# Attention with cached keys: every full matmul and transpose written as two of 64 output columns

## The chip, the cores and the metric

One core of a Trainium2 chip. The metric is the time of one execution on the device in microseconds; the kernel before takes 453.37 us (median of three runs, 451.6 to 454.62). Only the core's own engines work: TensorE (PE: matmuls, and its weight loads, PEld), VectorE (DVE), ScalarE (ACT), GpSimd (POOL, set-up only) and SyncE (SP, which issues all DMAs).

## The reference

```python
B, Sq, D = 8, 112, 640;  H, Sk, Dh = 32, 512, 192          # all bf16
q = (x @ wq).reshape(B, Sq, H, Dh).transpose(0, 2, 1, 3)
scores = jnp.einsum("bhqd,bhkd->bhqk", q, k_cache) * (Dh ** -0.5)
p = softmax(scores, axis=-1)
o = jnp.einsum("bhqk,bhkd->bhqd", p, v_cache)
return o.transpose(0, 2, 1, 3).reshape(B, Sq, H * Dh) @ wo
```

Eight batches of 112 queries, 32 heads, 512 cached keys and values of 192 elements per head.

## The kernel before

**Tiles and steps.** The heads are done in two halves of 16, and a (half, batch) is a time t, 16 in all. A step n (0 to 63) is four heads of one time. For each step TensorE does five things: the queries of two head pairs that a later step needs (`q_fill`, L329: weights `wq`, 224 columns of x streamed, that is two batches), the scores (`scores`), the transposes of the softmaxed probabilities (`transposes`, L447, eight per pair of heads), the values (`values`), and a part of the output projection (`o_half`, L520: weights `wo`, 224 columns streamed). Heads of 192 are cut as 128 + 64. For the scores, the 128-deep part are the matmuls of L384 and L386 (256 keys streamed, 112 output columns), and the 64-deep rests are L397 and L399, which use the two row halves of the array side by side. For the values, the 128-wide part is L486 (112 queries streamed), and the 64-wide rests are L475, for which the two heads of a pair use the two column halves of the array side by side: one writes partitions 0 to 63 of a PSUM bank, the other 64 to 127.

**Other uses of TensorE.** x and the keys of times 0 and 1 come in their natural order and are transposed on TensorE (`x_transposes` L281, `k_transposes` L295); the keys of later times are transposed by the DMA that loads them. The end of the program has its own pieces of the output projection (`o_six` L559, `o_last` L583) and transposes the result back (`o_final` L608). `idle` (L318) runs 22 matmuls on zeros at the start.

**Who reads the results.** ACT copies queries, half of the transposed probabilities and the values out of PSUM and computes the exponentials (L417); DVE finds the maxima of the scores (L412), normalizes (L421), copies the other half of the transposes (L453) and adds up the output projection (L536, L538).

**The order.** Nothing is scheduled by the machine. Each engine has a list of operations by name (`Plan.order`), written out by hand for the front (steps 0 to 8) and the tail (from step 58) and made by a loop between (steps 9 to 57). In the loop TensorE's list of a step n is: scores of n, values of n - 2, queries, first part of the output projection, transposes of n - 1, second part. Each operation names what it depends on. `Plan.run` turns the dependences into waits on semaphores: an operation adds one to its engine's semaphore when its last instruction ends, and readers wait for a count. An operation may also name two semaphores; `emit` then returns two instructions, each of which adds to one of them. Before the change that is so for the rests of the scores alone (`St`, L402: semaphores `PE` and `PE2`), whose two last matmuls run side by side.

**The matmul in the program.** Each `e.matmul(out, weights, moving)` and each `e.transpose(out, in, identity)` becomes two instructions of TensorE: a weight load and a matmul. No weights are used twice in a row.

Of the kernel before, what the change touches and what calls it, by code (L numbers as in the profile page):

```python
# [52 lines left out]
def build_mha_kernel(nc, x, k_cache, v_cache, wq, wo, out):  # L53
# [27 lines left out]
    with ExitStack() as es:  # L81
# [40 lines left out]

        P = Plan()
        add, order = P.add, P.order


        def k_done(t, lo, hi):
# [150 lines left out]
        def x_transposes(c, bank, eng):  # L278
            def emit(e):
                for dc in range(DC):  # L280
                    mm = e.transpose(psb[:, bank, dc * 128:(dc + 1) * 128], xn[c // 4][:, c % 4, dc * 128:(dc + 1) * 128],  # L281
                                     ident[:, :])
                return mm

            def evac(e):
                dst = xT_sb[:, :, c * 128:(c + 1) * 128]
                src = psb[:, bank, 0:D].rearrange("p (c s) -> p c s", c=DC)
                return e.activation(dst, src, ACTF.Copy) if eng == "ACT" else e.tensor_copy(dst, src)
            add("PE", ("XT", c), [x_piece[c]], emit)
            add(eng, ("evX", c), [("XT", c)], evac)  # L290

        def k_transposes(t, u, bank, eng):
            def emit(e):
                for c in range(6):
                    mm = e.transpose(psb[:, bank, c * 128:(c + 1) * 128], kn[:, u, c * 128:(c + 1) * 128], ident[:, :])  # L295
                return mm

            def evac(e):
                dst = kt[t][:].rearrange("p a m c -> p (a m) c")[:, :, u * 128:(u + 1) * 128]
                src = psb[:, bank, 0:768].rearrange("p (c r) -> p c r", c=6)  # L300
                return e.activation(dst, src, ACTF.Copy) if eng == "ACT" else e.tensor_copy(dst, src)
            add("PE", ("KT", t, u), [kn_of[t, u]], emit)
            add(eng, ("evK", t, u), [("KT", t, u)], evac)


# [15 lines left out]
        def q_fill(m, lp, part, bank):  # L321
            half, bp = divmod(m, B // 2)
            blocks = (0, 1) if part == "a" else (2,)

            def emit(e):
                for j, c in enumerate(blocks):
                    for dc in range(DC):
                        c0 = lp * 2 * DH + 128 * c
                        mm = e.matmul(ps[:, bank, j * S2:(j + 1) * S2], wq_sb[:, dc, c0:c0 + 128],  # L329
                                      xT_sb[:, dc, bp * S2:(bp + 1) * S2], start=(dc == 0), stop=(dc == DC - 1))  # L330
                return mm

            def evac(e):
                n = len(blocks)
                return e.activation(q_home(m, lp)[:, blocks[0]:blocks[0] + n, :],  # L335
                                    ps[:, bank, 0:n * S2].rearrange("p (c s) -> p c s", c=n), ACTF.Copy)

            old = []
            if m != 1 and q_seq.index((m, lp)) >= NQ:
                for n in q_last(*q_seq[q_seq.index((m, lp)) - NQ]):  # L340
                    old += [("St", n, 3), ("qc", n)]
            rows = range(bp * S2 // 128, (bp * S2 + S2 - 1) // 128 + 1)
            add("PE", ("Q" + part, m, lp), [wq_piece[half, lp]] + [("evX", c) for c in rows], emit)
            add("ACT", ("evQ" + part, m, lp), [("Q" + part, m, lp)] + old, evac)

        def q_of(n):
# [20 lines left out]
        def scores(n):  # L367
# [10 lines left out]
            for j in range(2):  # L378
                def emit(e, j=j):
                    for h in range(2):  # L380
                        i = 2 * j + h
                        ev, od = (raw(j, 0), qh[:, n % 2, j, 1, :]) if h == 0 else (qh[:, n % 2, j, 2, :], raw(j, 2))
                        hs = slice(h * 256, (h + 1) * 256)
                        e.matmul(ps[0:SQ, 2 * j, hs], ev, ktb[:, :, 0, cs(i)], start=(h == 0), stop=False,  # L384
                                 skip_group_check=True)
                        mm = e.matmul(ps[0:SQ, 2 * j + 1, hs], od, ktb[:, :, 2, cs(i)], start=(h == 0), stop=False,  # L386
                                      skip_group_check=True)
                    return mm
                add("PE", ("Sm", n, j), [("qc", n), ("smax", n - 1, 2 * j), ("smax", n - 1, 2 * j + 1)] +
                    ([("evK", t, 4 * s + i) for i in range(4)] if t < 2 else [k_piece[t, s]]), emit)  # L390
            for i in range(4):
                def emit(e, i=i):
                    j, h = divmod(i, 2)
                    ev, od = ((raw(j, 1)[0:64], qh[64:128, n % 2, j, 0, :]) if h == 0 else
                              (qh[0:64, n % 2, j, 3, :], raw(j, 1)[64:128]))
                    hs = slice(h * 256, (h + 1) * 256)
                    m1 = e.matmul(ps[0:SQ, 2 * j, hs], ev, ktb[0:64, :, 1, cs(i)], start=False, stop=True,  # L397
                                  skip_group_check=True)
                    m2 = e.matmul(ps[0:SQ, 2 * j + 1, hs], od, ktb[64:128, :, 1, cs(i)], start=False, stop=True,  # L399
                                  skip_group_check=True)  # L400
                    return m1, m2
                add("PE", ("St", n, i), [], emit, ("PE", "PE2"))  # L402

        def softmax(n):
            for i in range(4):
# [34 lines left out]
        def transposes(n, j):  # L440
            bank = end_bank.get(("PT", n, j), 4 + j)

            def emit(e):
                for h in range(2):
                    for q in range(4):
                        c = (4 * h + q) * SQ
                        mm = e.transpose(psb[:, bank, c:c + SQ], p_sb[:, (4 * n + 2 * j + h) % 8, q * 128:(q + 1) * 128],  # L447
                                         ident[0:SQ, 0:SQ])
                return mm

            def evac(e):
                dst, src = pT_sb[:, j, :, :].rearrange("p h c -> p (h c)"), psb[:, bank, 0:8 * SQ]
                return e.activation(dst, src, ACTF.Copy) if j == 0 else e.tensor_copy(dst, src)  # L453
            add("PE", ("PT", n, j), [("norm", n, 2 * j), ("norm", n, 2 * j + 1)] +
                ([("smax", n, i) for i in range(4)] if n == NN - 1 else []), emit)
            add("DVE" if j else "ACT", ("evPT", n, j), [("PT", n, j)] + ([] if n - 1 in BY_DMA else [("PVm", n - 1, j)]), evac)

        def values(n):
# [22 lines left out]
            for j in range(2):  # L481
                def mains(e, j=j):
                    for h in range(2):
                        for q in range(4):
                            d0 = QJ[q] * DH + 64 * h
                            mm = e.matmul(ps[:, b0 + j, 2 * h * SQ:(2 * h + 1) * SQ],  # L486
                                          vtb[:, h0 + 2 * j + h, d0:d0 + 128], pT(j, h, q),
                                          start=(q == 0), stop=(q == 3))
                    return mm
                add("PE", ("PVm", n, j), [], mains)  # L490

            u = t // 2 * 2 + s // 2

# [17 lines left out]
        def o_half(u, f, part):  # L511
# [5 lines left out]

            def emit(e):
                for j, m, k in todo:
                    mm = e.matmul(ps[:, o_bank(u, f), j * S2:(j + 1) * S2], wo_sb[:, KU * (u % 2) + k, m * 128:(m + 1) * 128],  # L520
                                  oT_sb[:, u % NO, k, :], start=(k == 0), stop=(k == KU - 1))
                return mm
            deps = []
            if part == 0 and f == 0:
                deps = ready(u) + [("WO", half, u % 2)]
            add("PE", ("O", u, f, part), deps, emit)

        def o_acc(u, f):
            half, bp = divmod(u // 2, B // 2)
# [23 lines left out]
        def o_six(g, part):  # L553

            def emit(e):
                for k in range(18, KB) if part else range(18):
                    w, o = wo_k(k)
                    for j, m in enumerate(SIX[g]):
                        mm = e.matmul(ps[:, end_bank["O6", g, 0], j * SQ:(j + 1) * SQ], w[:, m * 128:(m + 1) * 128], o[:, 0:SQ],  # L559
                                      start=(k == 0 and j == 0), stop=(k == KB - 1), skip_group_check=True)  # L560
                return mm
            add("PE", ("O6", g, part), [("evPV", step_of[NT - 2, 2 + part])], emit)

        def o_six_acc(g):
            m0, n = SIX[g][0], len(SIX[g])
# [8 lines left out]
        def o_last(s, part):  # L574
# [3 lines left out]
            def emit(e):  # L578
                for k in range(6 * s, 6 * s + 6):
                    w, o = wo_k(k)  # L580
                    for m in blocks:
                        bank, c = LAST[m]
                        mm = e.matmul(ps[:, bank, c * SQ:(c + 1) * SQ], w[:, m * 128:(m + 1) * 128], o[:, SQ:S2],  # L583
                                      start=(k == 0 and c == 0), stop=(k == KB - 1), skip_group_check=True)
                return mm
            add("PE", ("OL", s, part), [("evPV", step_of[NT - 1, s])], emit)

        def o_last_acc(part):
            def emit(e):
# [12 lines left out]
        def o_final(b):  # L602
# [2 lines left out]

            def emit(e):
                for m in range(DC):
                    mm = e.transpose(psb[0:SQ, bank, m * 128:(m + 1) * 128], oF[:, bp, m, bb * SQ:(bb + 1) * SQ, 0],  # L608
                                     ident[:, :])
                return mm  # L610

            def evac(e):
                return e.activation(xT_sb[0:SQ, b % DC, 0:D], psb[0:SQ, bank, 0:D], ACTF.Copy)
            need = [("oacc", 8 + 2 * bp + 1, f) for f in range(4)] if bp < BL else [("oaccL", 0), ("oaccL", 1)] if bb else [("oacc6", g) for g in range(3)]
            add("PE", ("OF", b), need, emit)
            add("ACT", ("oout", b), [("OF", b), ("Qb", NM - 1, LP - 1), ("OUT", b - DC)], evac)


# [322 lines left out]
```

## Time and profile before

| | |
|---|---|
| median of three runs | 453.37 us |
| the profiled execution's own time | 452.17 us |
| its span, first to last instruction | 450.2 us |
| granted TensorE clock | 0.999 |
| TensorE: matmuls, weight loads | 6,345 and 6,345 |
| idle time of DVE, of ACT | 82 us, 112 us |
| data moved by DMA | 121.94 MB, mean 271 GB/s |

How to read the profile. "PE" rows are matmuls, "PEld" rows weight loads; both belong to one engine with one sequencer. A form such as `128*64 128x112` means 128 rows and 64 columns of the array in use, and an output of 112 streamed columns. Matmuls are pipelined: a single one is shown 0.2 us long or longer, but the next one starts much earlier. What a matmul costs in a row of many is therefore the distance from one start to the next, and in a merged line of the order of time ("x16") it is the line's length, less one matmul's own, divided by the number less one. `[0.39 <-issue]` is idle time ahead of an instruction for which the profile shows no semaphore. In a table of stretches the columns are the stretch, its length, the busy time of PE, PEld, DVE, ACT and POOL with their instruction counts, the granted clock, the DMA share and GB/s. In the DMA part a queue has its packets, megabytes, and share of 16 engines' time; "instruction" is the kind of a queue that brings an engine's program. The trace also holds every single DMA packet with queue, start, duration and size.

### The profile page before, as it was taken

To read this page: it belongs to the slowest core of one execution; us is meant where nothing else is said; L and a number is where in the kernel's file an instruction comes from. 1 tells how busy PE (TensorE), PEld (TensorE's weight loads), DVE (VectorE), ACT (ScalarE), POOL (GpSimd) and SP (SyncE) were. 2 spreads that over 40 slices of the span, in tenths; PEclk is the share of its full clock that TensorE was granted. 3 is DMA by queue.
4 is the path that set the end of the run, shared out by engine and by line. 5 is a ranking of instruction groups with operands and counts; after the bars stand their busy time and mean duration, and the time that the engine had idled before them with its cause. 6 is when DMAs were issued, how large, how long until landed. Compare 5 with 4: busy or idle time off the path is not lost.

```text
span 450.2 us, 15025 instructions
## 1 busy us (share of the span) xinstructions
PE 438.4 (97%) x6345; PEld 402.8 (89%) x6345; DVE 367.8 (82%) x1172; ACT 338.4 (75%) x787; POOL 0.7 (0%) x6
## 2 busy tenths in 40 slices
PE   8999999999999999999999999998999999999996
PEld 7799888998998899999999999997999989999986
DVE  1788789979888988898898888887798888889961
ACT  3688898868767877787687778767678777867683
POOL 0000000000000000000000000000000000000000
PEclk9999999999999999999999999999999999999999
DMA  8999999999999999999999999999999999999972
GB/s 296 373 376 359 238 302 245 250 328 277 261 275 279 315 240 352 232 336 258 274 290 232 287 229 341 261 261 363 227 306 187 276 220 217 273 244 269 223 193 67
DMA packets 232547, 121.94 MB, mean 271 GB/s; under 512 B 182560, under 2 KB 232480, under 8 KB 232480
## 3 DMA queue, kind: packets, MB, share of 16 engines
q1 hardware_dynamic: 232480, 120.99, 110.6%
q8 instruction: 50, 0.82, 0.7%
q14 instruction: 17, 0.14, 0.1%
HBM read 73.50 MB, written 1.15 MB: 166 GB/s over the span
## 4 chain that ended last, share of the span: by engine, by line
PE 85%; DMA 6%; DVE 4%; ACT 4%; issue 1%; SPq 0%; DVEq 0%; ACTq 0%
PE ps L329 18%; PE ps L520 17%; PE ps L486 11%; PE ps L447 10%; PE ps L397 7%; PE ps L475 6%; PE ps L384 6%; PE ps L386 6%; DMA wo_sb<-in_wo_dram 3%; DVE s_sb L412 3%; ACT p_sb L417 2%; PE ps L295 2%; DMA wq_sb<-p_sb 1%; DMA wq_sb<-in_wq_dram 1%; PE ps L583 1%
## 5 line engine op out<-in xcount | busy, mean ns | idle before, releaser
L417 ACT ACTIVATE p_sb<-s_sb,nmx 112x512 bf16<-112x512 f32 x256 | 183.2, 716 | 83.2 <-DVE s_sb L412 79.7
L412 DVE TENSOR_SCALAR_CACHE_REDUCE s_sb<-ps 112x512 f32<-112x512 f32 x256 | 167.5, 688 | 40.4 <-ACT p_sb L417 19.4
L329 PE MATMUL ps<-xT_sb,wq_sb 128*128 128x224 bf16 x960 | 111.1, 259 | 0.6 <-issue 0.4
L520 PE MATMUL ps<-oT_sb,wo_sb 128*128 128x224 bf16 x840 | 96.6, 259 | 1.8 <-DMA wo_sb<-in_wo_dram 1.8
L329 PEld LDWEIGHTS ps<-xT_sb,wq_sb 128*128 128x128 bf16 x960 | 88.6, 98 | 2.1 <-issue 0.9
L421 DVE TENSOR_SCALAR p_sb<-p_sb,rinv 112x512 bf16<-112x512 bf16 x256 | 79.3, 350 | 3.9
L520 PEld LDWEIGHTS ps<-oT_sb,wo_sb 128*128 128x128 bf16 x840 | 78.3, 98 | 2.1 <-DMA wo_sb<-in_wo_dram 2.1
L335 ACT ACTIVATE qr<-ps 128x448 bf16<-128x448 f32 (+1 forms) x112 | 49.1, 442 | 15.7 <-PE ps L329 15.6
L447 PE MATMUL ps<-ident,p_sb 112*128 112x112 bf16 x944 | 57.2, 213 | 1.2 <-ACT oT_sb L496 0.9
L453 ACT ACTIVATE pT_sb<-ps 128x896 bf16<-128x896 bf16 x59 | 53.5, 906 | 1.8 <-PE ps L447 1.1
L486 PE MATMUL ps<-pT_sb,vt 128*128 128x112 bf16 x912 | 54.8, 213 | 0.0
L447 PEld LDWEIGHTS ps<-ident,p_sb 112*128 112x128 bf16 x944 | 51.5, 98 | 3.4 <-ACT oT_sb L496 2.6
L486 PEld LDWEIGHTS ps<-pT_sb,vt 128*128 128x128 bf16 x912 | 45.8, 98 | 4.5
L417 ACT ACTIVATION_READ_ACCUMULATOR p_sb<-s_sb,nmx 112x1 f32 x256 | 49.0, 191 | 0.0
L496 ACT ACTIVATE oT_sb<-ps 128x672 bf16<-128x672 f32 x64 | 45.6, 712 | 3.8 <-PE ps L486 3.8
L453 DVE COPY pT_sb<-ps 128x896 bf16<-128x896 bf16 x59 | 36.4, 617 | 5.2 <-PE ps L447 5.2
L384 PE MATMUL ps<-kt,qh 128*112 128x256 bf16 x128 | 34.9, 273 | 0.0
L386 PE MATMUL ps<-kt,qh 128*112 128x256 bf16 x128 | 34.9, 272 | 0.0
L475 PEld LDWEIGHTS ps<-pT_sb,vt 128*64 128x64 bf16 x912 | 24.9, 109 | 10.9 <-issue 9.6
L475 PE MATMUL ps<-pT_sb,vt 128*64 128x112 bf16 x912 | 33.3, 216 | 0.8 <-issue 0.6
L399 PE MATMUL ps<-kt,qh 64*112 64x256 bf16 x128 | 34.0, 291 | 0.0
L384 PE MATMUL ps<-kt,qr 128*112 128x256 bf16 x112 | 30.7, 274 | 1.9 <-DVE qh L362 1.0
(68 smaller groups left out, 506.5 us busy)
## 6 DMA issues: line engine op xcount, KB each, us to landing
vt<-in_v_cache_dram SPq DMA_DIRECT2D x31, 1536.0 KB, 8.4
wq_sb<-in_wq_dram SPq DMA_DIRECT2D x8, 960.0 KB, 9.6
wo_sb<-in_wo_dram SPq DMA_DIRECT2D x4, 1920.0 KB, 13.0
wo_sb<-in_k_cache_dram SPq DMA_DIRECT2D x3, 1536.0 KB, 12.7
wo_sb<-in_k_cache_dram SPq DMA_DIRECT2D x2, 768.0 KB, 8.8
wq_sb<-in_v_cache_dram SPq DMA_DIRECT2D x1, 1536.0 KB, 8.0
out_dram<-xT_sb SPq DMA_DIRECT2D x8, 140.0 KB, 2.4
oT_sb<-in_x_dram SPq DMA_DIRECT2D x2, 320.0 KB, 8.9
```

Source lines behind the costliest of these rows:

```text
L329: mm = e.matmul(ps[:, bank, j * S2:(j + 1) * S2], wq_sb[:, dc, c0:c0 + 128], xT_sb[:, dc, bp * S2:(bp + 1) * S2], start=(dc == 0), stop=(d ...
L335: return e.activation(q_home(m, lp)[:, blocks[0]:blocks[0] + n, :], ps[:, bank, 0:n * S2].rearrange("p (c s) -> p c s", c=n), ACTF.Copy)
L384: e.matmul(ps[0:SQ, 2 * j, hs], ev, ktb[:, :, 0, cs(i)], start=(h == 0), stop=False, skip_group_check=True)
L386: mm = e.matmul(ps[0:SQ, 2 * j + 1, hs], od, ktb[:, :, 2, cs(i)], start=(h == 0), stop=False, skip_group_check=True)
L412: return e.tensor_scalar(s_sb[:, a, :].rearrange("p (e c) -> p e c", e=2), ps[0:SQ, 2 * j:2 * j + 2, h * 256:(h + 1) * 256], -scale, None, ...
L417: return e.activation(p_sb[:, k, :], s_sb[:, a, :], ACTF.Exp, bias=nmx[:, k:k + 1], scale=-1.0, accum_out=rsum[:, k:k + 1])
L421: return e.tensor_scalar(p_sb[:, k, :], p_sb[:, k, :], rinv[:, k:k + 1], None, op0=ALU.mult)
L447: mm = e.transpose(psb[:, bank, c:c + SQ], p_sb[:, (4 * n + 2 * j + h) % 8, q * 128:(q + 1) * 128], ident[0:SQ, 0:SQ])
L453: return e.activation(dst, src, ACTF.Copy) if j == 0 else e.tensor_copy(dst, src)
L475: mm = e.matmul(ps[64 * h:64 * h + 64, b0 + j, SQ:2 * SQ], vtb[:, h0 + 2 * j + h, d0:d0 + 64], pT(j, h, q), start=(q == 0), stop=(q == 3))
L486: mm = e.matmul(ps[:, b0 + j, 2 * h * SQ:(2 * h + 1) * SQ], vtb[:, h0 + 2 * j + h, d0:d0 + 128], pT(j, h, q), start=(q == 0), stop=(q == 3))
L520: mm = e.matmul(ps[:, o_bank(u, f), j * S2:(j + 1) * S2], wo_sb[:, KU * (u % 2) + k, m * 128:(m + 1) * 128], oT_sb[:, u % NO, k, :], start ...
```

## The change

Two helpers issue each matmul, or transpose, as two: the weights' columns 0 to 63 into partitions 0 to 63 of the bank, columns 64 to 127 (or to 111, where only 112 are used) into partitions 64 to 127, with the same moving operand. All matmuls and transposes use them except the rests of the scores (L397, L399), the rests of the values (L475, which already have this form) and the idle matmuls (L318). As the last two matmuls of an operation now run on different halves of the array, both are returned, and the operation adds to both semaphores, `PE` and `PE2`; readers wait for both. The order of the operations, the DMAs, the tiles and the other engines' work stay as they are.

```diff
+        BOTH = ("PE", "PE2")
+
+        def halves(e, bank, rows, cols, w, moving, **kw):
+
+            return tuple(e.matmul(bank[64 * h:min(64 * h + 64, rows), cols], w[:, 64 * h:min(64 * h + 64, rows)], moving, **kw)
+                         for h in range(2))
+
+        def flip(e, bank, rows, cols, src, unit):
+
+            return tuple(e.transpose(bank[64 * h:min(64 * h + 64, rows), cols], src[:, 64 * h:min(64 * h + 64, rows)], unit)
+                         for h in range(2))
...
-                        mm = e.matmul(ps[:, bank, j * S2:(j + 1) * S2], wq_sb[:, dc, c0:c0 + 128],
-                                      xT_sb[:, dc, bp * S2:(bp + 1) * S2], start=(dc == 0), stop=(dc == DC - 1))
+                        mm = halves(e, ps[:, bank, :], 128, slice(j * S2, (j + 1) * S2), wq_sb[:, dc, c0:c0 + 128],
+                                    xT_sb[:, dc, bp * S2:(bp + 1) * S2], start=(dc == 0), stop=(dc == DC - 1))
                 return mm
...
-            add("PE", ("Q" + part, m, lp), [wq_piece[half, lp]] + [("evX", c) for c in rows], emit)
+            add("PE", ("Q" + part, m, lp), [wq_piece[half, lp]] + [("evX", c) for c in rows], emit, BOTH)
...
-                        e.matmul(ps[0:SQ, 2 * j, hs], ev, ktb[:, :, 0, cs(i)], start=(h == 0), stop=False,
-                                 skip_group_check=True)
+                        halves(e, ps[:, 2 * j, :], SQ, hs, ev, ktb[:, :, 0, cs(i)], start=(h == 0), stop=False,
+                               skip_group_check=True)
...
-                        mm = e.transpose(psb[:, bank, c:c + SQ], p_sb[:, (4 * n + 2 * j + h) % 8, q * 128:(q + 1) * 128],
-                                         ident[0:SQ, 0:SQ])
+                        mm = flip(e, psb[:, bank, :], 128, slice(c, c + SQ),
+                                  p_sb[:, (4 * n + 2 * j + h) % 8, q * 128:(q + 1) * 128], ident[0:SQ, 0:SQ])
...
-                            mm = e.matmul(ps[:, b0 + j, 2 * h * SQ:(2 * h + 1) * SQ],
-                                          vtb[:, h0 + 2 * j + h, d0:d0 + 128], pT(j, h, q),
-                                          start=(q == 0), stop=(q == 3))
+                            mm = halves(e, ps[:, b0 + j, :], 128, slice(2 * h * SQ, (2 * h + 1) * SQ),
+                                        vtb[:, h0 + 2 * j + h, d0:d0 + 128], pT(j, h, q),
+                                        start=(q == 0), stop=(q == 3))
```

The other matmuls and transposes (x, the keys of times 0 and 1, L386, the output projection in all its parts, the transposes of the result) are rewritten in the same way.

More of the change, by code (lines that the diff above doesn't have):

```diff
@@ L280, in emit @@
                 for dc in range(DC):
-                    mm = e.transpose(psb[:, bank, dc * 128:(dc + 1) * 128], xn[c // 4][:, c % 4, dc * 128:(dc + 1) * 128],
-                                     ident[:, :])
+                    mm = flip(e, psb[:, bank, :], 128, slice(dc * 128, (dc + 1) * 128),
+                              xn[c // 4][:, c % 4, dc * 128:(dc + 1) * 128], ident[:, :])
                 return mm
@@ L288, in evac @@
                 return e.activation(dst, src, ACTF.Copy) if eng == "ACT" else e.tensor_copy(dst, src)
-            add("PE", ("XT", c), [x_piece[c]], emit)
+            add("PE", ("XT", c), [x_piece[c]], emit, BOTH)
             add(eng, ("evX", c), [("XT", c)], evac)
@@ L294, in emit @@
                 for c in range(6):
-                    mm = e.transpose(psb[:, bank, c * 128:(c + 1) * 128], kn[:, u, c * 128:(c + 1) * 128], ident[:, :])
+                    mm = flip(e, psb[:, bank, :], 128, slice(c * 128, (c + 1) * 128),
+                              kn[:, u, c * 128:(c + 1) * 128], ident[:, :])
                 return mm
@@ L301, in evac @@
                 return e.activation(dst, src, ACTF.Copy) if eng == "ACT" else e.tensor_copy(dst, src)
-            add("PE", ("KT", t, u), [kn_of[t, u]], emit)
+            add("PE", ("KT", t, u), [kn_of[t, u]], emit, BOTH)
             add(eng, ("evK", t, u), [("KT", t, u)], evac)
@@ L383, in emit @@
                         hs = slice(h * 256, (h + 1) * 256)
-                        e.matmul(ps[0:SQ, 2 * j, hs], ev, ktb[:, :, 0, cs(i)], start=(h == 0), stop=False,
-                                 skip_group_check=True)
-                        mm = e.matmul(ps[0:SQ, 2 * j + 1, hs], od, ktb[:, :, 2, cs(i)], start=(h == 0), stop=False,
-                                      skip_group_check=True)
+                        halves(e, ps[:, 2 * j, :], SQ, hs, ev, ktb[:, :, 0, cs(i)], start=(h == 0), stop=False,
+                               skip_group_check=True)
+                        mm = halves(e, ps[:, 2 * j + 1, :], SQ, hs, od, ktb[:, :, 2, cs(i)], start=(h == 0), stop=False,
+                                    skip_group_check=True)
                     return mm
                 add("PE", ("Sm", n, j), [("qc", n), ("smax", n - 1, 2 * j), ("smax", n - 1, 2 * j + 1)] +
-                    ([("evK", t, 4 * s + i) for i in range(4)] if t < 2 else [k_piece[t, s]]), emit)
+                    ([("evK", t, 4 * s + i) for i in range(4)] if t < 2 else [k_piece[t, s]]), emit, BOTH)
             for i in range(4):
@@ L401, in emit @@
                     return m1, m2
-                add("PE", ("St", n, i), [], emit, ("PE", "PE2"))
+                add("PE", ("St", n, i), [], emit, BOTH)
         def softmax(n):
@@ L454, in transposes @@
             add("PE", ("PT", n, j), [("norm", n, 2 * j), ("norm", n, 2 * j + 1)] +
-                ([("smax", n, i) for i in range(4)] if n == NN - 1 else []), emit)
+                ([("smax", n, i) for i in range(4)] if n == NN - 1 else []), emit, BOTH)
             add("DVE" if j else "ACT", ("evPT", n, j), [("PT", n, j)] + ([] if n - 1 in BY_DMA else [("PVm", n - 1, j)]), evac)
@@ L485, in mains @@
                             d0 = QJ[q] * DH + 64 * h
-                            mm = e.matmul(ps[:, b0 + j, 2 * h * SQ:(2 * h + 1) * SQ],
-                                          vtb[:, h0 + 2 * j + h, d0:d0 + 128], pT(j, h, q),
-                                          start=(q == 0), stop=(q == 3))
+                            mm = halves(e, ps[:, b0 + j, :], 128, slice(2 * h * SQ, (2 * h + 1) * SQ),
+                                        vtb[:, h0 + 2 * j + h, d0:d0 + 128], pT(j, h, q),
+                                        start=(q == 0), stop=(q == 3))
                     return mm
-                add("PE", ("PVm", n, j), [], mains)
+                add("PE", ("PVm", n, j), [], mains, BOTH)
             u = t // 2 * 2 + s // 2
@@ L519, in emit @@
                 for j, m, k in todo:
-                    mm = e.matmul(ps[:, o_bank(u, f), j * S2:(j + 1) * S2], wo_sb[:, KU * (u % 2) + k, m * 128:(m + 1) * 128],
-                                  oT_sb[:, u % NO, k, :], start=(k == 0), stop=(k == KU - 1))
+                    mm = halves(e, ps[:, o_bank(u, f), :], 128, slice(j * S2, (j + 1) * S2),
+                                wo_sb[:, KU * (u % 2) + k, m * 128:(m + 1) * 128],
+                                oT_sb[:, u % NO, k, :], start=(k == 0), stop=(k == KU - 1))
                 return mm
@@ L525, in o_half @@
                 deps = ready(u) + [("WO", half, u % 2)]
-            add("PE", ("O", u, f, part), deps, emit)
+            add("PE", ("O", u, f, part), deps, emit, BOTH)
         def o_acc(u, f):
@@ L558, in emit @@
                     for j, m in enumerate(SIX[g]):
-                        mm = e.matmul(ps[:, end_bank["O6", g, 0], j * SQ:(j + 1) * SQ], w[:, m * 128:(m + 1) * 128], o[:, 0:SQ],
-                                      start=(k == 0 and j == 0), stop=(k == KB - 1), skip_group_check=True)
+                        mm = halves(e, ps[:, end_bank["O6", g, 0], :], 128, slice(j * SQ, (j + 1) * SQ),
+                                    w[:, m * 128:(m + 1) * 128], o[:, 0:SQ],
+                                    start=(k == 0 and j == 0), stop=(k == KB - 1), skip_group_check=True)
                 return mm
-            add("PE", ("O6", g, part), [("evPV", step_of[NT - 2, 2 + part])], emit)
+            add("PE", ("O6", g, part), [("evPV", step_of[NT - 2, 2 + part])], emit, BOTH)
         def o_six_acc(g):
@@ L582, in emit @@
                         bank, c = LAST[m]
-                        mm = e.matmul(ps[:, bank, c * SQ:(c + 1) * SQ], w[:, m * 128:(m + 1) * 128], o[:, SQ:S2],
-                                      start=(k == 0 and c == 0), stop=(k == KB - 1), skip_group_check=True)
+                        mm = halves(e, ps[:, bank, :], 128, slice(c * SQ, (c + 1) * SQ), w[:, m * 128:(m + 1) * 128],
+                                    o[:, SQ:S2], start=(k == 0 and c == 0), stop=(k == KB - 1), skip_group_check=True)
                 return mm
-            add("PE", ("OL", s, part), [("evPV", step_of[NT - 1, s])], emit)
+            add("PE", ("OL", s, part), [("evPV", step_of[NT - 1, s])], emit, BOTH)
         def o_last_acc(part):
@@ L607, in emit @@
                 for m in range(DC):
-                    mm = e.transpose(psb[0:SQ, bank, m * 128:(m + 1) * 128], oF[:, bp, m, bb * SQ:(bb + 1) * SQ, 0],
-                                     ident[:, :])
+                    mm = flip(e, psb[:, bank, :], SQ, slice(m * 128, (m + 1) * 128), oF[:, bp, m, bb * SQ:(bb + 1) * SQ, 0],
+                              ident[:, :])
                 return mm
@@ L614, in o_final @@
             need = [("oacc", 8 + 2 * bp + 1, f) for f in range(4)] if bp < BL else [("oaccL", 0), ("oaccL", 1)] if bb else [("oacc6", g) for g in range(3)]
-            add("PE", ("OF", b), need, emit)
+            add("PE", ("OF", b), need, emit, BOTH)
             add("ACT", ("oout", b), [("OF", b), ("Qb", NM - 1, LP - 1), ("OUT", b - DC)], evac)
```

## The prediction

> **What bounds the kernel now.** I read the page's head first, then its chain, then the trace's order of time, and last the DMA queues.
>
> ```profile
> span 450.2 us, 15025 instructions
> PE 438.4 (97%) x6345; PEld 402.8 (89%) x6345; DVE 367.8 (82%) x1172; ACT 338.4 (75%) x787; POOL 0.7 (0%) x6
> PE 85%; DMA 6%; DVE 4%; ACT 4%; issue 1%; SPq 0%; DVEq 0%; ACTq 0%
> q8 instruction: 50, 0.82, 0.7%
> ```
>
> TensorE is busy or being handed work all the time and carries 85% of the chain. Only 18 pairs of neighbouring matmuls start more than 250 ns apart after the first 4 us, and the largest of these waits (2.1 us, 1.3 us, 1.1 us) are single events. So a nanosecond saved or lost between two matmuls counts nearly in full. Whether busy TensorE time is useful time is seen in one step (columns: start, duration, line, operation, shape, count):
>
> ```profile
> 202.88 0.27 PE L384 MATMUL ps<-kt,qh 128*112 128x256 bf16 x1
> 202.99 0.27 PE L386 MATMUL ps<-kt,qr 128*112 128x256 bf16 x1
> 203.19 0.31 PE L397 MATMUL ps<-kt,qr 64*112 64x256 bf16 x1
> ...
> 203.46 0.27 PE L397 MATMUL ps<-kt,qr 64*112 64x256 bf16 x1
> ...
> 203.56 0.27 PE L397 MATMUL ps<-kt,qh 64*112 64x256 bf16 x1
> 203.57 0.27 PE L399 MATMUL ps<-kt,qr 64*112 64x256 bf16 x1
> 203.77 0.58 PE L475 MATMUL ps<-pT_sb,vt 128*64 128x112 bf16 x16
> 204.28 0.96 PE L486 MATMUL ps<-pT_sb,vt 128*128 128x112 bf16 x16
> ```
>
> Within one shape, starts are 0.11 us apart at 256 streamed columns. Where the shape changes they are 0.20 apart (L386 to L397) and 0.21 apart (L399 to L475): a change of the array's partition costs about 0.1 us. The same rows price the new form. L475 is already two matmuls of 64 output columns side by side: 16 of them in 0.58 us, the last 0.216 long, so (0.58 - 0.216) / 15 = 24.3 ns each and **48.6 ns a pair**. L486, full width over the same 112 columns, takes (0.96 - 0.213) / 15 = **49.8 ns each**. A pair costs what a full matmul costs.
>
> **The change, part by part.**
>
> *Fewer changes of shape: about -7.6 us.* A score step now goes full, 64-row halves (L397, L399), then, with the values right behind it, 64-column halves (L475), full (L486): three changes. Afterwards everything but L397/L399 and the idle matmuls of L318 is in 64-column form, so two remain. From single records: full to row halves 92 ns in the gap plus 44 in the slower second start; row to column halves 92 + 25; column halves to full 99 + 11. I take 110 ns for one that goes. All 64 value steps lose one; the eight that stand apart from a score step in the written order (three in the front, five in the tail) lose a second: 72, less 3 new ones around L318: 69 x 0.110 = 7.6. What is late next is TensorE itself, so nearly all of it shows; were DVE or ACT last in some steps, less (0 to -7.6).
>
> *4,787 matmuls and as many weight loads more.* 6,345 less L475 (1,024), L397/L399 (512) and L318 (22) are split. Array time: nothing at 112 columns by the two rows above. For 224 and 256 columns no 64-column pair is in the trace; the nearest row is the pair of row halves (L397 with L399), which goes through 256 columns in 0.105 us, a full matmul's 0.11. I take nothing; bounds -1.2 ns a pair (L486 against L475, -6 us over 4,787) and +1 ns (+5).
>
> *Dispatch.* Half the duration per instruction could strike TensorE's sequencer. One L475 group began with nothing queued, at 74.66 after a 0.6 us gap: its 32 instructions started within 0.40 us, 12.6 ns each, the pace of the groups that had been queued. The densest new stretch (four instructions per 48.6 ns) needs 12.2. Nothing, then; bound +3% of the 112- and 128-column work, +3 us.
>
> *Weight loads.* A load of 128 columns takes 98 ns, the 64-column one of L475 109, and both lie under matmuls; the pair above holds its 48.6 ns with two new loads each time. The Trainium skill, "TensorEngine Tiling (Array Packing)", section "Feature Incompatibilities", says that column tiling excludes the fast weight load, which speaks against this change. By that rule alone loads would come to set the pace; the L475 row shows a longer load and no slower pair, so by the row the term is zero.
>
> *Second wait.* Every reader of a split result waits for two semaphores. Some 270 ACT and 145 DVE instructions may get one more wait record; such a record takes 51 ns on PE: 14 us and 7 us against 112 and 82 us of idle time there. Behind one queues the rest of its engine, and PE waits for that only where it is already close (PE waits on ACT and DVE for about 10 us in all). 0 to +2 us; I take 0.
>
> *Instruction supply: the term that decides.* Queue q8 has 50 packets of 16,384 bytes each, 0.82 MB. TensorE has 12,690 matmuls and loads plus some 170 waits and others, 257 for each packet: q8 feeds TensorE's sequencer, one page of 256 instructions (64 bytes each) at a time. Now a page lasts 450.2 / 50 = 9.0 us. After the change there are 12,690 + 9,574 + about 170 = 22,430 instructions, 87.6 pages, over 450.2 - 7.6 = 442.6 us: **5.05 us a page**. What does fetching one take? The trace shows one late page:
>
> ```profile
> 370.04 0.64 PE L329 MATMUL ps<-xT_sb,wq_sb 128*128 128x224 bf16 x5
> 371.07 0.64 PE L329 MATMUL ps<-xT_sb,wq_sb 128*128 128x224 bf16 x5 [0.39 <-issue]
> ```
>
> Ten matmuls of one accumulation, no semaphore between, and the sixth starts 0.64 us after the fifth instead of 0.096. It is the instruction just past record 10,432 of TensorE's; with 64 records' offset, page boundary 41. The packet fetched before it is the latest of all 50: it started 5.9 us after TensorE had crossed boundary 40, took 1.18 us (landed 369.60), and work resumed 1.47 us later. So a page is requested when the one before it is entered, and no page further ahead is in hand. Measured so, the other packets start -0.1 to 5.9 us after the crossing, mean of the first 48 2.88, and take 1.03; the two after the loads had ended (439 us on) start at 0.34 and -0.06. The delay is time spent among 121 MB of other packets.
>
> Crossing to usable is thus 2.88 + 1.03 + 1.47 = 5.4 us on average, now under 9.0 (one stall in 50), then against 5.05. Taking the 48 delays one by one, the mean of the larger of 5.05 and (delay + 1.03 + 1.47) is 5.78: 0.73 x 87.6 = **+64 us**. Lower end: work resumes 0.9 us after landing, +36. Upper end: the sequencer runs some 32 instructions ahead of the array (at 202.1 it waits for L475's data while L384 starts), 1.1 us, which a sequencer that has just been starved no longer has; then +134. Against the upper end: a longer run thins the other traffic. I let these two cancel and keep +64.
>
> *The same fetches seen by the loads.* Key transposes move 290 GB/s, but not while a page is fetched (last column; fetches at 206.80 and 213.68):
>
> ```profile
> 207.00:208.00 1.00, 1.00 (x21) 1.00 (x19) 0.96 (x4) 1.00 (x4) 0.00 (x0) 1.00 2.20 74
> 210.00:211.00 1.00, 1.00 (x28) 0.92 (x27) 0.99 (x3) 0.25 (x1) 0.00 (x0) 1.00 1.27 290
> 214.00:215.00 1.00, 1.00 (x17) 1.00 (x15) 0.99 (x3) 1.00 (x4) 0.00 (x0) 1.00 1.82 45
> ```
>
> Each costs 1.3 to 2 us of transposing. Keys land about 6 us before use in a 26 us cycle; 2.5 more fetches there take 3 to 5 of that. Nothing by itself, and little is left.
>
> Sum: 450.2 - 7.6 + 64 = 506.6, and 2.0 around the span (452.17 - 450.2): 508.6. The profiled run lies 1.2 below the median of 453.37, which I don't add.
>
> **The rivals.**
>
> *The fetch stays hidden: faster, 444.6* (442.6 + 2.0; with the array's bounds 438 to 449). For it: one stall of 0.6 us in all of the kernel. Against it: that stall's place and time. It decides if a request comes two pages early, or delay, transfer and resumption stay under 5.05 us; then only the shape changes are left. The Trainium skill, "Runtime: NRT & Kernel Launch", section "Instruction fetch mechanics", stands on this side: pages of 256 instructions are fetched while the current one runs, and crossing a boundary is "mostly hidden". That holds in this trace at 9 us a page, 49 times in 50.
>
> *Partly hidden: 455 to 490.* The delays fall as requests meet lighter traffic: with delays 1 us shorter throughout, the larger-of-two mean falls to about 5.3, +23 us: 468.
>
> *Keys late as well: 570 and more.* Over half of all fetches would have to fall into transposes, each with 2 us: 87.6 x 2 less the present 50 x 2 and 14 x 6 of slack is below zero, so only on top of the upper end, 442.6 + 134 + 2 = 579.
>
> *It doesn't do what it says:* halves that run one after the other. 4,787 more matmuls at 50 to 107 ns, beyond 700; L475's row excludes it.
>
> **How the numbers follow.** Fetch-bound, 490 to 570: 0.58. Partly hidden, 455 to 490: 0.20. Hidden and faster: 0.16. Hidden, the gain eaten by waits, 449 to 455: 0.03. Over 570: 0.03. To leave out no more than 2 in 10 the range goes from 451 to 570. About 1% is what a measurement of this kernel can tell from no change: faster than 448.8 0.16, within 1% 0.04, slower than 457.9 0.80. The likeliest case's own range is 479 to 570.
>
> **What would show it.** q8: some 87 packets. Gaps of 0.5 us and more between matmuls with no wait, "issue" as the releaser, one page apart, with q8's packets landing 1 to 1.5 us before each ends; the chain's "issue" or sequencer share well above 1%. L486 and L329 pairs keep 49 and 96 ns. L397 stays the only place with 0.1 us gaps, 128 times and not 192. TensorE's busy share falls, DVE and ACT idle more. Wrong if those gaps are missing (then near 445), or if pairs at 224 columns are slower than 97 ns.

## The result and the profile after

The changed kernel takes **534.98 us** (median; 532.79 to 537.96), the kernel before 452.34 beside it (449.68 to 454.62): 1.183 times as long, 95% interval 1.177 to 1.188. The forecast was 508.6 with a range of 451 to 570. The profiled execution's span is 533.4 us against 450.2: 83.2 us more.

The page of the changed kernel (head, granted clock, instruction queue, chain):

```profile
span 533.4 us, 24991 instructions
PE 453.2 (85%) x11132; PEld 412.5 (77%) x11132; DVE 370.4 (69%) x1172; ACT 343.0 (64%) x787; POOL 0.7 (0%) x6
PEclk9999789899898999999999999998999999999999
q8 instruction: 87, 1.43, 1.1%
PE 79%; issue 13%; ACT 2%; DMA 2%; DVE 2%; SPq 0%; DVEq 0%; ACTq 0%
```

TensorE's busy time hardly grew (438.4 to 453.2) for 1.75 times the matmuls, so the pairs do lie side by side. Its share fell from 97% to 85%, queue q8 brings 87 pages for 50, and "issue", time for which the profile shows no semaphore, is now 13% of the chain, where it was 1%. DVE and ACT were not slowed; they wait more for TensorE. In the order of time (start, duration, line, operation, count, idle time ahead) the lost time looks like this:

```profile
54.02 0.53 PE L129 MATMUL ps<-xT_sb,wq_sb 128*64 128x224 bf16 x3 [3.46 <-issue]
54.21 0.56 PE L129 MATMUL ps<-kt,qr 128*64 128x256 bf16 x2
54.43 0.77 PE L129 MATMUL ps<-kt,qh 128*64 128x256 bf16 x4
54.85 0.77 PE L129 MATMUL ps<-kt,qr 128*64 128x256 bf16 x4
...
227.77 0.93 PE L129 MATMUL ps<-oT_sb,wo_sb 128*64 128x224 bf16 x16
231.12 0.29 PE L129 MATMUL ps<-oT_sb,wo_sb 128*64 128x224 bf16 x2 [2.41 <-issue]
```

After 228.45 the next pair of the output projection is not there; it starts 2.67 us after the one before. The stalled instruction is record 9,153 of TensorE's, with the offset of 63 that the one stall of the kernel before gives, 36 x 256 exactly. The page that was missing began to arrive at 228.87, had landed at 229.81, and work went on 1.30 us later. Counted over the whole trace, 52 of the 87 page boundaries have a gap of more than 0.4 us from one matmul's start to the next, together **82.9 us** (1.7 us of it are the ordinary distances). Every one of them ends 1.25 to 1.60 us after its packet has landed (mean 1.42). The few gaps over 0.4 us elsewhere are waits for other engines and for loads, such as the kernel before has too.

These lines show a second thing. From 54.2 on pairs of 256 columns start 0.21 us apart instead of 0.109 (four matmuls, 0.77 long, the next group 0.42 later). The clock column of the table of stretches says why (stretch, length, busy PE, PEld, DVE, ACT, POOL, granted clock, DMA share, GB/s):

```profile
53.00:60.00 7.00, 5.97 (x87) 5.21 (x88) 2.58 (x8) 1.52 (x4) 0.00 (x0) 0.54 1.24 230
```

### The profile page after: what moved, and what is told of

It is laid out like the page before. It is cut to its first block, busy times and chain, and to the rows that moved or that the text cites. A ratio compares the mean times of both kernels' runs of the same rounds, so it can differ in the third digit from the quotient of the medians.

```text
span 533.4 us, 24991 instructions
## 1 busy us (share of the span) xinstructions
PE 453.2 (85%) x11132; PEld 412.5 (77%) x11132; DVE 370.4 (69%) x1172; ACT 343.0 (64%) x787; POOL 0.7 (0%) x6
## 4 chain that ended last, share of the span: by engine, by line
PE 79%; issue 13%; ACT 2%; DMA 2%; DVE 2%; SPq 0%; DVEq 0%; ACTq 0%
PE ps L129 54%; PE ps L134 12%; PE ps L409 7%; PE ps L487 6%; DMA wo_sb<-in_k_cache_dram 2%; ACT p_sb L429 1%; DVE s_sb L424 1%; PE ps L411 0%; ACT oT_sb L508 0%; ACT pT_sb L465 0%; DVE p_sb L433 0%; SPq L209 0%; DVE accT L606 0%; ACT kt L313 0%; ACT xT_sb L627 0%
## 5 line engine op out<-in xcount | busy, mean ns | idle before, releaser
L129 PE MATMUL ps<-oT_sb,wo_sb 128*64 128x224 bf16 (+1 forms) x2160 | 116.5, 252 | 15.4 <-issue 15.4
L129 PE MATMUL ps<-xT_sb,wq_sb 128*64 128x224 bf16 x1920 | 117.3, 264 | 12.4 <-issue 10.7
L129 PEld LDWEIGHTS ps<-oT_sb,wo_sb 128*64 128x64 bf16 x2160 | 95.5, 111 | 18.2 <-issue 18.2
L129 PEld LDWEIGHTS ps<-xT_sb,wq_sb 128*64 128x64 bf16 x1920 | 94.4, 112 | 15.5 <-issue 12.5
L347 ACT ACTIVATE qr<-ps 128x448 bf16<-128x448 f32 (+1 forms) x112 | 49.1, 442 | 46.5 <-PE ps L129 46.3
L134 PE MATMUL ps<-ident,p_sb 112*64 112x112 bf16 x1888 | 60.9, 214 | 13.5 <-issue 10.8
L134 PEld LDWEIGHTS ps<-ident,p_sb 112*64 112x64 bf16 x1888 | 53.3, 110 | 17.4 <-issue 12.0
L129 PE MATMUL ps<-pT_sb,vt 128*64 128x112 bf16 x1824 | 58.5, 218 | 9.1 <-issue 9.1
L129 PE MATMUL ps<-kt,qr 128*64 128x256 bf16 (+1 forms) x448 | 56.6, 276 | 4.4 <-issue 3.3
L129 PEld LDWEIGHTS ps<-pT_sb,vt 128*64 128x64 bf16 x1824 | 51.6, 114 | 10.0 <-issue 10.0
L129 PE MATMUL ps<-kt,qh 128*64 128x256 bf16 (+1 forms) x512 | 53.3, 278 | 2.8 <-issue 2.8
L487 PE MATMUL ps<-pT_sb,vt 128*64 128x112 bf16 x912 | 35.6, 221 | 8.3 <-issue 8.3
L487 PEld LDWEIGHTS ps<-pT_sb,vt 128*64 128x64 bf16 x912 | 26.5, 113 | 18.6 <-issue 17.9
```

The lines of the kernel that those rows point to most:

```text
L129: return tuple(e.matmul(bank[64 * h:min(64 * h + 64, rows), cols], w[:, 64 * h:min(64 * h + 64, rows)], moving, **kw) for h in range(2))
L134: return tuple(e.transpose(bank[64 * h:min(64 * h + 64, rows), cols], src[:, 64 * h:min(64 * h + 64, rows)], unit) for h in range(2))
L487: mm = e.matmul(ps[64 * h:64 * h + 64, b0 + j, SQ:2 * SQ], vtb[:, h0 + 2 * j + h, d0:d0 + 64], pT(j, h, q), start=(q == 0), stop=(q == 3))
```

## The experiments

Theory: the extra time is instruction supply. A page of 256 instructions is requested when TensorE enters the one before (the crossing of a page boundary), waits among the other DMA packets, and is late once TensorE uses a page faster than that takes. Rivals: the column halves cost time themselves (on the array, in dispatch, or by the second semaphore), which gives a price per split matmul; or any traffic would do, or one kind of it.

### 1 and 2: the loads left out

The same edit in both kernels, after all operations are in the lists:

```diff
+        LEFT_OUT = ([("K", t, 0) for t in range(4, NT)] + [("V", t, lo) for t in range(4, NT) for lo in (0, 8) if (t, lo) != (NT - 1, 8)])
+        for name in LEFT_OUT:
+            order["SP"].remove(name)
+            del P.ops[name]
         P.number()
```

> Leaves out the loads of keys and of values from time 4 on (all but the last unit of values), so the results from there on are those of older tiles. Instruction supply theory: TensorE's pages are fetched through the same DMA engines as the loads; with little traffic a page comes 0.3 to 1 us after the crossing, and 1.1 + 1.4 more make it usable within 3.5 us, under the 5.06 us that a page lasts. The stalls at page boundaries all but vanish and the 7.6 us of saved shape changes come out: 443 to 449 us. Rival, the halves are slow on the array or in the sequencer by themselves: nothing changes, 515 us or more.

> The control: the kernel before with the same loads left out. It hardly stalls now, so it loses its one late page (0.6 us) and at most the waits for loads of about 4 us: 447 to 453 us. What the one without loads is faster than this is the worth of the shape changes, 5 to 8 us by the prediction, nothing or less if the halves cost array time.

Measured: the changed kernel without these loads 469.45 us (1.036 times the kernel before beside it, 1.029 to 1.043), the kernel before without them 448.64 (0.990, 0.987 to 0.994). The control did as expected; the other lies between both expectations, 20 us above the upper end of the theory's. The page of the changed kernel without the loads says where:

```profile
span 470.0 us, 24925 instructions
DMA  8998965997340201212000050220000000015642
q8 instruction: 87, 1.43, 1.3%
PE 87%; issue 5%; DMA 3%; ACT 2%; DVE 2%; SPq 0%; DVEq 0%; ACTq 0%
```

The loads of times 0 to 3 are still there, and they fill the DMA engines up to the tenth slice, some 120 us; the expectation had overlooked that. Up to 125 us there are 19.0 us of stalls, as in the changed kernel itself (18.3). Between 125 and 420 us, with the DMA engines nearly idle, **one** of 58 pages is late (1.6 us), where the changed kernel has 30 of 48 and 49.6 us. The mean delay from a crossing to the start of the fetch is 0.38 us there against 3.11. The number of instructions and the halves are the same in both, so neither makes the stalls alone; the traffic does it with them.

The undisturbed stretch also shows what the shape changes were worth. A step without stalls takes 6.153 us here and 6.232 in the control; the longer kind, with a larger piece of the projection, 7.276 and 7.382. That is 79 to 106 ns a step, some 5.5 us over 64. The order of time shows the two changes of shape that are left and the one that is gone:

```profile
302.10 0.28 PE L129 MATMUL ps<-kt,qr 128*64 128x256 bf16 x2
302.30 0.31 PE L409 MATMUL ps<-kt,qr 64*112 64x256 bf16 x1
...
302.68 0.27 PE L409 MATMUL ps<-kt,qh 64*112 64x256 bf16 x1
302.68 0.27 PE L411 MATMUL ps<-kt,qr 64*112 64x256 bf16 x1
302.88 0.58 PE L487 MATMUL ps<-pT_sb,vt 128*64 128x112 bf16 x16
303.30 0.90 PE L129 MATMUL ps<-pT_sb,vt 128*64 128x112 bf16 x30
```

0.20 us into the row halves and 0.20 out of them, as before. But L487's last pair starts at 303.25 and the full value block follows at 303.30, 49 ns on, where there were 148.

### 3 and 4: fewer matmuls split

The kernel before with the new helpers, first for the value matmuls of 128 columns alone (1,024), then also for the first part of the queries and of each projection piece (2,174):

```diff
-                            mm = e.matmul(ps[:, b0 + j, 2 * h * SQ:(2 * h + 1) * SQ],
-                                          vtb[:, h0 + 2 * j + h, d0:d0 + 128], pT(j, h, q),
-                                          start=(q == 0), stop=(q == 3))
+                            mm = halves(e, ps[:, b0 + j, :], 128, slice(2 * h * SQ, (2 * h + 1) * SQ),
+                                        vtb[:, h0 + 2 * j + h, d0:d0 + 128], pT(j, h, q),
+                                        start=(q == 0), stop=(q == 3))
```

> The kernel before with the 1,024 value matmuls of 128 columns alone split; still three shape changes in a step. 58 pages of 7.7 us. Instruction supply: only the latest few of the fetches miss their page, +1 to +3 us: 451 to 457. Rival, a fixed price for each split matmul (91 us over 4,787, 19 ns each): +19 us, 471.

> The kernel before with 2,174 matmuls split: the values of 128 columns, the first part of the queries and the first part of each piece of the output projection, which follow each other in the loop, so that a step keeps three shape changes (some more in front and tail, +3 to +5 us). 67 pages of 6.7 us. Instruction supply: 9 to 12 us of stalls at page boundaries, 463 to 470. Rival, a fixed price for each split: +41 us, 495 with the shapes.

Measured: 453.54 us with 1,024 split, no difference (1.0003, 0.997 to 1.003), and 466.97 with 2,174 (1.029, 1.022 to 1.037). Both lie in the theory's ranges, neither at a fixed price per split. The pages of the first,

```profile
span 450.3 us, 17197 instructions
q8 instruction: 58, 0.95, 0.8%
```

and of the second:

```profile
span 466.2 us, 19556 instructions
q8 instruction: 67, 1.10, 1.0%
```

At boundaries the first has one stall, 1.0 us; the second eleven, 14.3 us, somewhat more than the 9 to 12 expected. With the kernel before and the changed one that makes a curve: **50 pages 0.6 us of stalls, 58 pages 1.0, 67 pages 14.3, 87 pages 82.9**. It is flat down to 7.8 us a page (450.3 us for 58) and steep at 6.7 (466.2 us less the stalls for 67), as a limit on time per page gives it and a price per instruction does not.

### 5: empty instructions

Two empty instructions (`e.nop()`) ahead of each matmul of queries, projection and 128-deep scores, in the kernel before.

> The kernel before, nothing split, with two empty instructions on TensorE ahead of each of the 2,312 matmuls of the queries, the output projection and the 128-deep scores: 17,500 instructions, 68 pages of 6.6 us. Instruction supply: the pages are late as in the kernel with 2,174 matmuls split (67 pages, 14 us of stalls at page boundaries), 462 to 468 us, with gaps only every 256 instructions, each ending some 1.4 us after its packet has landed. Rival, it is the halves that cost: 450 to 454. Should an empty instruction take some 50 ns of the sequencer, the 224-column matmuls would be spaced by over 100 ns instead of 96 everywhere, which the order of time would show.

Measured: 452.03 us (1.001, 0.998 to 1.003). But the page shows that the empty instructions never reached the program:

```profile
span 450.2 us, 15025 instructions
q8 instruction: 50, 0.82, 0.7%
```

The same 15,025 instructions and 50 pages as before. It tells nothing of either theory.

### 6 and 7: which traffic

The changed kernel with the edit of experiment 1 for the keys alone, and for the values alone.

> The changed kernel without the loads (by transposing DMA) of keys from time 4 on; values, weights and the rest are loaded. In the changed kernel the fetches that waited beside transposes led to 45 of the 83 us of stalls, those beside plain loads to 31. If transposes delay a page as a kind of traffic of their own, their stalls go and those beside the values stay: 40 to 55 us of stalls, 490 to 505. If any traffic delays alike by how much of the time it is there, about the same. If only transposes delay: 24 us of stalls, 470, as without loads.

> The changed kernel without the loads of values from time 4 on (but the last unit); keys are loaded. If transposes delay more (4.0 us against 2.7 from the crossing to the start of the fetch, in the changed kernel): 60 to 75 us of stalls, 505 to 525, slower than without keys. If plain loads delay more, faster than that.

Measured: 470.42 us without keys (1.043, 1.037 to 1.048), 493.51 without values (1.094, 1.088 to 1.099). Chains without keys,

```profile
span 468.0 us, 24967 instructions
PE 87%; issue 5%; ACT 3%; DMA 3%; DVE 1%; SPq 0%; DVEq 0%; ACTq 0%
```

and without values:

```profile
span 491.7 us, 24959 instructions
PE 84%; issue 9%; DMA 2%; ACT 2%; DVE 2%; SPq 0%; DVEq 0%; ACTq 0%
```

Without keys I had expected 490 to 505: wrong; it stops at the time of no loads at all, the third case named there. Without values it is slower than without keys, as expected of transposes that delay more, but the 505 to 525 and the 60 to 75 us of stalls expected were too high as well: there are 49.1. In the stretch from 125 to 420 us the stalls are 1.6 us without both, 3.3 with values only, 24.9 with keys only, 49.6 with both. The runs with one kind each move about the same there, 148 and 150 GB/s. With values only, 5 of the 29 fetches that met load packets led to a stall, after a mean delay of 1.6 us; with keys only, 18 of 33, after 2.9. So the transposing loads delay the pages far more; plain loads do little alone in this stretch, and double the stalls beside the transposes. That plain loads do nothing would be too much: the first transposing packet of the changed kernel comes at 48 us, and yet, with plain loads alone moving 375 GB/s between 20 and 34.5 us, its pages are late at 28.1 us (0.5 us) and at 34.7 (1.9). Without keys the same two are late, by 0.6 and 1.6 us. Whether plain loads later act by their own packets, or by leaving the transposes no gaps, these runs don't separate.

### 8: more instructions without halves

The kernel before in full width, the streamed columns cut in two instead (also for the 128-deep scores, 256 into two of 128):

```diff
-                        mm = e.matmul(ps[:, bank, j * S2:(j + 1) * S2], wq_sb[:, dc, c0:c0 + 128],
-                                      xT_sb[:, dc, bp * S2:(bp + 1) * S2], start=(dc == 0), stop=(dc == DC - 1))
+                        for g in range(2):
+                            mm = e.matmul(ps[:, bank, j * S2 + g * SQ:j * S2 + (g + 1) * SQ], wq_sb[:, dc, c0:c0 + 128],
+                                          xT_sb[:, dc, bp * S2 + g * SQ:bp * S2 + (g + 1) * SQ],
+                                          start=(dc == 0 and g == 0), stop=(dc == DC - 1), skip_group_check=True)
```

> The kernel before, all in full width, with each matmul of the queries, the output projection and the 128-deep scores cut in the streamed columns instead (224 into two of 112, 256 into two of 128; the weights are loaded twice): 2,312 matmuls and loads more, 17,480 instructions, 68 pages, and no column halves but the old ones. On the array two full matmuls of 112 columns cost 99.6 ns for 96 and two of 128 cost 111 for 109, +8 us. Instruction supply theory: on top of that late pages as in the kernel with 67 pages (14 us of stalls there), 8 to 16 us: 466 to 476, each stall ending some 1.4 us after a page has landed and 256 instructions apart. Rival, the column halves or their second semaphore make the stalls: 457 to 461 and no such gaps.

Measured: 473.87 us (1.052, 1.045 to 1.058), inside the theory's range. 16 stalls at boundaries, 15.8 us, each ending 1.27 to 1.60 us after its packet had landed; steps without a stall are 0.09 us longer (6.32 against 6.23), the array's part. Page and order of time:

```profile
span 470.9 us, 19649 instructions
q8 instruction: 68, 1.11, 1.0%
PE 89%; ACT 3%; issue 3%; DVE 2%; DMA 2%; SPq 0%; DVEq 0%
```

```profile
188.98 0.51 PE L330 MATMUL ps<-xT_sb,wq_sb 128*128 128x112 bf16 x7
191.31 0.31 PE L330 MATMUL ps<-xT_sb,wq_sb 128*128 128x112 bf16 x3 [1.82 <-issue]
```

Full-width matmuls, one semaphore, and the same stall in the middle of an accumulation. 68 pages give 15.8 us here and 67 pages 14.3 with column halves: it is the count that matters.

## Why the prediction was right, and where its sizes were off

**Instruction supply, +64: right in kind, too small, measured 82.9.** The page period without stalls came out at 5.06 us (forecast 5.05), the number of pages at 87 (87.6), the transfer at 1.09 us (1.03), the time from landing to work at 1.42 (1.47 from one case). The term that was mis-sized is the delay to the start of the fetch: I took the 48 delays of the kernel before, one by one. Their mean was nearly right, 2.95 us measured for 2.88, but the new ones spread more (median 3.4 for 2.9), and only the long ones cost time. With the changed kernel's own delays, transfers, 1.42 and 5.06 the forecast's larger-of-two mean gives 82 us in place of 64. After a crossing without a stall the delay is 2.47, after one with a stall 3.27. That is the upper end's argument: a sequencer that has just been starved has no lead over the array, and asks later. Where no load packet ran between crossing and fetch, it stands alone: in the changed kernel and its three runs with loads left out, 20 such fetches after a stall started 1.25 us after the crossing, 105 after none 0.28, near the 1.1 us of lead that the upper end assumed. Under load the two are mixed with the traffic that they meet, and the difference is smaller beside one kind: 3.9 against 3.5 us beside transposes, 2.9 against 2.7 beside plain loads. I had let the lost lead cancel against thinner traffic; the traffic did not thin enough (DMA moves 230 GB/s for 271, and the engines are busy in most slices).

**Shape changes, -7.6: about -5.5,** from steps without stalls. The change that goes gives back 99 ns, as the rows said; in the shorter kind of step 20 ns of it are lost again elsewhere.

**Array time, 0: right.** Pairs of 224 columns start 95 to 97 ns apart, of 256 columns 109, of 112 columns 49; L475's row held for the two widths of which no pair had been seen. **Dispatch and weight loads, 0: right,** by the same spacings. The rule of the Trainium skill weighed there, in "TensorEngine Tiling (Array Packing)", section "Feature Incompatibilities", changed nothing at these widths: loads take 111 ns for 98 and stay hidden.

**Second wait, 0: right.** ACT now has 227 more wait records and DVE 132 (some 270 and 145 were forecast), and the undisturbed steps of experiment 1, which have these waits too, are shorter than the control's.

**Left out: the clock.** Half speed is granted for 27.3 us of the span (0.9 before), in windows of 3.41 us or twice that, each beginning in a stall of 2.1 us or more or within 1.2 us of its end; 7 of the 15 stalls of 2 us or more did it. 25 us of it are outside the gaps, worth up to 12.5. The Trainium skill, "TensorE: Matmul & The Clock Gate", section "HAM oscillation — how this bites in real kernels", says that TensorE idle for a window of some 3.4 us falls back to half its clock. A length of 3.41 us is what the half-speed stretches here have, but less idle time sufficed. Which stalls do it can be read from the traces: the half-speed stretches of a run begin whole multiples of 3.41 us apart, and what counts is how much of a gap between two matmul starts falls into one cell of that grid. In the nine profiles (the kernel before, the changed one and the experiments except the empty instructions), after the first 9 us, each of the 12 gaps with more than 2.1 us in one cell was followed by half speed at the cell's end, none of the 53 gaps over 1.5 us with at most 2.01 in a cell was, and of three between one was. So the run without keys had a gap of 3.2 us, at most 1.8 of it in one cell, and kept its clock.

**The sum.** 450.2 - 5.5 + 82.9 = 527.6; to 533.4 there remain 5.8 us, or 7.5 without the 1.7 of ordinary distances in the gaps. The clock can have cost up to 12.5; the waits that the loads bring the kernel before, 3.5 us by experiment 2, can now lie under stalls. How much each is was not separated.

**The rivals.** The hidden fetch, 444.6, with the Trainium skill's "mostly hidden" ("Runtime: NRT & Kernel Launch", section "Instruction fetch mechanics") on its side: refuted at 5 us a page under load, right at 7.8 us a page (one of 58 late) and without traffic (one of 58 late at 5 us). Its condition, crossing to usable within a page's time, was the right one. Partly hidden, with delays 1 us shorter: on average they stayed as they were (2.95 us for 2.88). Late keys: no wait for a transposed key tile stands among the long gaps.

No kernel tried here that computes the whole result beats the one before. The shape changes are worth 1.2% only where pages come in time, and in the kernel before transposing loads run in about half of the microseconds, other loads in most of the rest.

## What to carry to other kernels

Splitting TensorE's work into more, smaller instructions has a price that no row of the array shows: 256 instructions must last longer than the fetch of the next 256. In the changed kernel that fetch, from crossing to usable, took 5.5 us on average (2.95 + 1.09 + 1.42) and 6.3 beside transposing loads (3.8 to the start of the fetch), some 21 to 25 ns an instruction, weight loads and matmuls counted together; with nearly idle DMA engines 3 us, some 12. Look for it as "issue" in the middle of an accumulation, at every 256th instruction, and in the packets of the instruction queue. Column halves themselves are free at the widths measured here, 112 to 256 streamed columns, and a change of the array's shape costs 0.1 us.

## What was unexpected

The transposing loads and the page fetches hold each other up. Where transposing loads moved more than plain ones, the loads' rate fell from 273 GB/s in the microsecond before a fetch to 116 in its first microsecond, on average over 36 fetches of the changed kernel, and from 278 to 130 over 30 of the kernel before; where plain loads moved more, from 334 to 201 over 35 fetches of the changed kernel. And between 125 and 420 us the loads of keys alone brought the stalls back by half, those of values alone to a fifteenth.
